# Pairing the third 128-token blocks from the first tile on in a fused attention and MLP kernel

## The chip, the cores and the metric

One core of a Trainium2 chip. The metric is device time in microseconds (us) of one execution. "Median" is over several executions, with the range behind it. "Span" is the profiled time from the first to the last instruction, some 2 us less. The granted clock is the share of TensorE's full clock that the profile records as granted: 1.00 is full, 0.50 half. All runs timed in rounds count as fast ones.

## The reference, cut to what matters

```python
# attention (RWKV-6): batch 4, heads 8, sequence 768, head size 48
for t in range(S):
    cur = einsum('bhd,bhe->bhde', u * k_t, v_t)
    y[:, :, t] = einsum('bhd,bhde->bhe', r_t, state + cur)
    state = w_t[..., None] * state + einsum('bhd,bhe->bhde', k_t, v_t)
x = y.transpose(0, 2, 1, 3).reshape(3072, 384)
# MLP: w_in is 384 x 2048, w_out is 2048 x 384
out = gelu_exact(x @ w_in) @ w_out
```

All is fp32. The kernel works through the 3072 tokens in eight tiles of T = 384, so three blocks of 128 tokens each.

## The kernel before: the parts that matter

While the MLP of tile x-1 runs, step by step, the attention of tile x is issued between its steps, in "slots". `place` says after which MLP step each slot comes; `place_next` does the same for the first two slots of tile x+1. In the traces an engine runs its own instructions in the order of issue (in `shift`, below, TensorE stood from 143.90 us on for two GELUs, and these ran only at 145.57, behind copies at which ScalarE had stood 3.76 us), so `place` sets who waits for whom.

```python
for x in range(1, NX):
    place = [1, 3, ..., 26, 32] if x == 1 else [1, 6, 8, 13, 15, 16, 18, 18, 20, 21]
    place_next = [38, 47] if x == 1 else [21, 24] if x % 2 == 0 else [25, 27]
    ...
    for step, _ in enumerate(mlp(x - 1)):
        if x == 1 and step == 2 * NF - 2:
            make_quarter_masks()
            more = w_sums()          # eight VectorE sums of w_out, needed from tile 1 on
        next(more, None)
        ...                          # weight conversion, loads of tile x + 1
        while place and place[0] <= step:
            place.pop(0)
            next(slots, None)
```

The second layer of the MLP multiplies two blocks at once in the manner of Strassen: seven products of eight matmuls of half width (128x192; in the profile before 56 of them take 18.21 us, 0.325 us each), where the plain way takes 32 matmuls of 128x384 (16 take 10.32 us, 0.645 us each), worth eight products. The first two blocks of a tile are paired with each other (not in tile 0, where the sums of `w_out` are not ready). The third blocks are paired over two tiles. The earlier tile "waits": it multiplies its block in two products. The later one "ends" the pair in five.

```python
def mlp(x):
    waits, ends = x % 2 == 1 and x < NX - 1, x % 2 == 0 and x > 0
    ...
    if final:           # tile 7: its third block alone, 16 matmuls of 128x384
        ...
    if halves:          # tiles 1 to 7: first two blocks, seven products
        ...
    if waits:           # two products on the third block
        ...
    elif ends:          # five more, and the results of both third blocks
        ...
    elif not final:     # tile 0: two blocks plainly, then the third alone
        ...
```

The "quarter products" L521 of tile 2 read `kx`, which VectorE's L500 writes last, after copies of ScalarE (L494):

```python
plain(FINE)             # ScalarE, L494
lay_out(FINE)           # VectorE, L499 and L500
yield                   # the slot at step 6 ends here; the products come at step 8
for h in QUARTERS:
    ...                 # TensorE: L514, then L521
```

A later slot transposes k: VectorE writes blocks (L473), twelve transfers of 48 KB move them (L468, eight issued by SyncE, four by ScalarE), and the k-v products (L598) read them.

## Time and profile before

| | before |
|---|---|
| time, median of 3 (range) | 604.82 us (604.36 to 607.17) |
| span of the profiled run | 601.6 us |
| mean granted TensorE clock | 1.000 |
| TensorE, VectorE, ScalarE busy | 98%, 78%, 30% |

Busy shares are averages over stages with different limits. Up to about 110 us VectorE converts the weights and is the bound (busy 9.76 to 9.86 of each 10 us from 60 to 110). From 170 us on TensorE runs with hardly a gap (none over 0.6 us in this profile).

### The profile page before, as it was taken

The numbers are of one execution on the slowest core, as the hardware profiler recorded it, in microseconds if no ns is written. First come the engines' busy times: TensorE is split into PE (matmuls) and PEld (weight loads), VectorE is DVE, ScalarE is ACT, GpSimd is POOL, SyncE is SP. The second block draws the span as 40 slices with busy tenths as digits, with TensorE's granted clock in tenths as the row PEclk, the third lists the DMA queues.
The fourth block names the chain that finished last, engine by engine and source line by source line (L and its number), as shares of the span: only waits on it lengthen the run. The fifth ranks groups of instructions, "written<-read, shape, count | busy, mean of one in ns | idle before, by whom it ended". The sixth has DMA issues, their size and how long they took to land.

```text
span 601.6 us, 16117 instructions
## 1 busy us (share of the span) xinstructions
PE 586.7 (98%) x6993; PEld 455.5 (76%) x7008; DVE 468.4 (78%) x896; ACT 178.9 (30%) x414; POOL 8.4 (1%) x24
## 2 busy tenths in 40 slices
PE   8779999999999999999999999999999999999997
PEld 4556566656798669986699568995689668999977
DVE  8979999998866978488884987679786888665701
ACT  2446476213223322213222232113222133024400
POOL 3100000000000000000000000000000000000000
PEclk9999999999999999999999999999999999999999
DMA  5775348111141305203052304213052002010000
GB/s 201 253 239 194 110 162 297 38 46 60 25 123 45 92 2 111 73 21 93 1 112 73 99 1 83 87 36 92 3 111 73 8 1 40 16 38 8 1 14 26
DMA packets 50566, 46.72 MB, mean 78 GB/s; under 512 B 31680, under 2 KB 35904, under 8 KB 50496
## 3 DMA queue, kind: packets, MB, share of 16 engines
q1 hardware_dynamic: 33152, 29.31, 15.8%
q10 hardware_dynamic: 17344, 16.39, 10.1%
q8 instruction: 55, 0.90, 0.6%
q14 instruction: 15, 0.12, 0.1%
HBM read 36.24 MB, written 4.72 MB: 68 GB/s over the span
## 4 chain that ended last, share of the span: by engine, by line
PE 71%; DMA 1%; issue 0%; DVE 0%; ACTq 0%
PE o_ps L888 30%; PE h_ps L874 26%; PE b L828 5%; PE d L521 4%; PE o_ps L917 2%; PE kv_ps L598 2%; PE y_ps L639 2%; PE y_ps L677 1%; DMA rkw<-kx 1%; PE d L514 1%; DVE o_sb L960 0%; ACTq L468 0%
## 5 line engine op out<-in xcount | busy, mean ns | idle before, releaser
L874 PE MATMUL h_ps<-xT,w_in_sb 128*128 128x384 f32 x672 | 223.0, 489 | 0.0
L874 PEld LDWEIGHTS h_ps<-xT,w_in_sb 128*128 128x128 f32 x672 | 125.9, 190 | 84.6 <-ACT xT L684 0.4
L877 ACT ACTIVATE g<-h_ps 128x384 f32<-128x384 f32 (+1 forms) x112 | 49.4, 443 | 168.3 <-PE h_ps L874 168.3
L888 PE MATMUL o_ps<-t,s 128*128 128x192 f32 x480 | 81.9, 329 | 0.0
L888 PEld LDWEIGHTS o_ps<-t,s 128*128 128x128 f32 x480 | 77.8, 190 | 0.7
L552 DVE COPY_PREDICATED a_sb<-quarter,d 128x384 f32<-128x384 uint8 (+2 forms) x108 | 45.1, 438 | 2.5
L888 PE MATMUL o_ps<-w_out_sb,g 128*128 128x192 f32 x224 | 38.7, 326 | 0.0
L888 PEld LDWEIGHTS o_ps<-w_out_sb,g 128*128 128x128 f32 x224 | 37.0, 190 | 1.9
L613 DVE SCALAR_TENSOR_TENSOR st<-st,tot_sb,kv_ps 128x48 f32<-128x48 f32 x160 | 29.0, 259 | 4.1 <-PE kv_ps L598 4.1
L1011 PE MATMUL o_ps<-w_out_sb,g 128*128 128x384 f32 x96 | 32.2, 491 | 0.0
L888 PE MATMUL o_ps<-w_out_sb,s 128*128 128x192 f32 x160 | 28.3, 330 | 0.0
L888 PE MATMUL o_ps<-t,g 128*128 128x192 f32 x160 | 27.6, 326 | 0.0
L408 PEld LDWEIGHTS d<-rkw 64*64 64x64 f32 x1152 | 18.6, 134 | 11.8 <-DVE rkw L443 7.8
L1011 PEld LDWEIGHTS o_ps<-w_out_sb,g 128*128 128x128 f32 x96 | 17.8, 190 | 12.3 <-DVE o_sb L1017 0.6
L345 DVE TRANSPOSE_TENSOR_REDUCE rkw<-kx 128x48 f32<-128x1536 f32 (+3 forms) x24 | 26.8, 1155 | 0.2
L521 PEld LDWEIGHTS d<-kx,rkw 64*64 64x64 f32 x1152 | 24.3, 133 | 3.4 <-DVE a_sb L559 1.6
L521 PE MATMUL d<-kx,rkw 64*64 64x96 f32 x1152 | 26.5, 245 | 0.0
L888 PEld LDWEIGHTS o_ps<-t,g 128*128 128x128 f32 x160 | 26.3, 190 | 0.0
L888 PEld LDWEIGHTS o_ps<-w_out_sb,s 128*128 128x128 f32 x160 | 25.9, 190 | 0.4
L408 PE MATMUL d<-rkw 64*64 64x64 f32 (+1 forms) x1152 | 20.9, 221 | 4.6 <-DVE rkw L443 2.9
L534 DVE TENSOR_TENSOR rkw<-rkw,tot_sb 128x768 f32<-128x768 f32 x12 | 11.5, 958 | 17.4 <-PE d L521 17.4
L381 DVE TENSOR_TENSOR rkw<-rkw 128x384 f32<-128x384 f32 (+2 forms) x24 | 23.6, 1004 | 0.4
(148 smaller groups left out, 741.8 us busy)
## 6 DMA issues: line engine op xcount, KB each, us to landing
rkw<-in_rkw_dram ACTq DMA_DIRECT2D x45, 256.0 KB, 2.8
raw<-in_w_out_dram SPq DMA_DIRECT2D x8, 768.0 KB, 4.4
out_dram<-o_sb SPq DMA_DIRECT2D x21, 192.0 KB, 1.9
raw<-in_w_in_dram SPq DMA_DIRECT2D x5, 768.0 KB, 6.0
v_in<-in_v_dram ACTq DMA_DIRECT2D x5, 584.0 KB, 3.7
raw<-in_w_in_dram SPq DMA_DIRECT2D x9, 256.0 KB, 3.8
rkw<-in_rkw_dram SPq DMA_DIRECT2D x8, 288.0 KB, 3.4
rkw<-in_rkw_dram SPq DMA_DIRECT2D x9, 256.0 KB, 7.5
```

What stands on the lines that cost most here:

```text
L345: nc.vector.tensor_reduce(out=fine_sb[:, e, 0:n].rearrange("p a n -> p (a n)"), in_=kx[:, o:o + n * n_m].rearrange("p (m j) -> p m j", j=3 ...
L381: nc.vector.tensor_mul(z, z, by)
L408: nc.tensor.matmul(d[half[p], g, n * width:(n + 1) * width], lhsT=kc[half[g], b, i, p], rhs=right(half[g], b, i, p), start=True, stop=True)
L521: nc.tensor.matmul(d[half[p], g, i * 3 * C // 2:(i + 1) * 3 * C // 2], lhsT=kc[half[g], (n + i) // NI, (n + i) % NI, p], rhs=rx[half[g], 2 ...
L552: nc.vector.copy_predicated(out=an[:, :, :, :, (a + 1) * h:], mask=mask.to_broadcast(data.shape), data=data)
L598: nc.tensor.matmul(kv_ps[half[g], p, i * D:(i + 1) * D], lhsT=k_t(b, i, p, g), rhs=vs(b, i, g)[half[p], 0:D], start=True, stop=True)
L613: nc.vector.scalar_tensor_tensor(out=stq[:, q, c], in0=stq[:, q, c - 1] if c else b4[:, q, NC - 1], scalar=totq[:, q, c:c + 1], in1=kvs[q ...
L828: nc.tensor.matmul(o, lhsT=lhsT, rhs=rhs, start=start and i == 0, stop=(i == len(factors) - 1), skip_group_check=True)
L874: nc.tensor.matmul(h_ps, lhsT=w_in_sb[:, f // FI, j, f % FI * 128:(f % FI + 1) * 128], rhs=xT[:, j, :], start=(j == 0), stop=(j == NJ - 1))
L877: nc.scalar.activation(out=gs[group][:, f % FG, 0:t], in_=h_ps[:, 0:t], func=AF.Gelu)
L888: nc.tensor.matmul(o, lhsT=lhs(j), rhs=rhs(j), start=start and j == 0, stop=(j == HF - 1), skip_group_check=True)
L1011: nc.tensor.matmul(o, lhsT=block(i, f // HF, f % HF), rhs=w_out_sb[:, f, :], start=(f == 0), stop=(f == NF - 1))
```

## The change

The intent: the third blocks of tiles 0 and 7 are multiplied alone, 16 full matmuls each. If tile 0 pairs with 1, 2 with 3 and so on, no block is alone, and the two cost seven products instead of eight. Tiles 1 to 6 swap roles, tile 0 now waits and tile 7 ends a pair. So the slots, the loads of tile 2, the sums of the weights (which now run over into the next tile) and the sums for the last tile are moved too. The diff, cut:

```diff
-            if i < 3:
-                yield
+            yield                        # h_sums: the last four adds get a slot of their own
...
-        waits, ends = x % 2 == 1 and x < NX - 1, x % 2 == 0 and x > 0
+        waits, ends = x % 2 == 0, x % 2 == 1
...
-        if final:                        # tile 7's third block alone: gone
...
+        else:                            # tile 0: two blocks plainly, 16 steps
+            ...
         if waits:                        # now also in tile 0
-            _, o2, o1 = psum(), psum(), psum()
+            if halves:
+                psum()
+            o2, o1 = psum(), psum()
...
-        elif not final:                  # tile 0's third block alone: gone
...
+    more = iter(())                      # moved out of the loop below
     for x in range(1, NX):
-        place = [..., 18, 20, 26, 32] if x == 1 else [1, 6, 8, ...]
-        place_next = [38, 47] if x == 1 else [21, 24] if x % 2 == 0 else [25, 27]
+        place = [..., 18, 20, 24, 28] if x == 1 else [1, 6, 8, ...]
+        place_next = [30, 33] if x == 1 else [25, 27] if x % 2 == 0 else [21, 24]
...
-        more = iter(())
...
-                for _ in range({18: 1, 22: 2, 25: 1}.get(step, 0)):
+                for _ in range({18: 1, 20: 1, 22: 1, 23: 1, 24: 1}.get(step, 0)):
                     next(more_h)
```

More of the change, by code (lines that the diff above doesn't have):

```diff
@@ L910, in two_rows @@
             return [wk.tile([128, DM], F32, name="o_sb", bufs=2) for _ in range(2)]
-        if final:
-            o_ps = ps.tile([128, BANK], F32, name="o_ps", tag="mm", bufs=2)[:, 0:DM]
-            order = [f for f in range(NF) if f % HF < HF - 1] + [HF - 1, NF - 1]
-            for n, f in enumerate(order):
-                nc.tensor.matmul(o_ps, lhsT=block(2, f // HF, f % HF), rhs=w_out_sb[:, f, :], start=(n == 0), stop=(n == NF - 1))
-            o_sb = wk.tile([128, DM], F32, name="o_sb", bufs=2)
-            nc.scalar.copy(out=o_sb, in_=o_ps)
-            store(x * T + 256, o_sb)
-            yield
+        row0 = x * T
         if halves:
-            row0 = x * T
             o_sb = two_rows()
@@ L966, in mlp @@
             yield
+        else:
+            o_ps = [ps.tile([128, BANK], F32, name="o_ps", tag="mm", bufs=2)[:, 0:DM] for _ in range(2)]
+            for f in range(NF):
+                for i, o in enumerate(o_ps):
+                    nc.tensor.matmul(o, lhsT=block(i, f // HF, f % HF), rhs=w_out_sb[:, f, :], start=(f == 0), stop=(f == NF - 1))
+                if f < NF - 1:
+                    yield
+            for i, o in enumerate(o_ps):
+                o_sb = wk.tile([128, DM], F32, name="o_sb", bufs=2)
+                nc.vector.tensor_copy(out=o_sb, in_=o)
+                store(row0 + i * 128, o_sb)
+            yield
         if waits:
-            _, o2, o1 = psum(), psum(), psum()
+            if halves:
+                psum()
+            o2, o1 = psum(), psum()
             o_sb = wk.tile([128, DM], F32, name="o_sb", bufs=2)
@@ L1004, in mlp @@
             yield
-        elif not final:
-            for blocks in (0, 1), (2,):
-                o_ps = [ps.tile([128, BANK], F32, name="o_ps", tag="mm", bufs=2)[:, 0:DM] for _ in blocks]
-                for f in range(NF):
-                    for i, o in zip(blocks, o_ps):
-                        nc.tensor.matmul(o, lhsT=block(i, f // HF, f % HF), rhs=w_out_sb[:, f, :],
-                                         start=(f == 0), stop=(f == NF - 1))
-                    if f < NF - 1:
-                        yield
-                for i, o in zip(blocks, o_ps):
-                    o_sb = wk.tile([128, DM], F32, name="o_sb", bufs=2)
-                    nc.vector.tensor_copy(out=o_sb, in_=o)
-                    store(x * T + i * 128, o_sb)
-                yield
     units = [attention(0, unit) for unit in range(units_of(0))]
@@ L1052 @@
     next(slots)
+    more = iter(())
     for x in range(1, NX):
-        place = [1, 3, 5, 7, 9, 11, 13, 15, 18, 20, 26, 32] if x == 1 else [1, 6, 8, 13, 15, 16, 18, 18, 20, 21]
-        place_next = [38, 47] if x == 1 else [21, 24] if x % 2 == 0 else [25, 27]
+        place = [1, 3, 5, 7, 9, 11, 13, 15, 18, 20, 24, 28] if x == 1 else [1, 6, 8, 13, 15, 16, 18, 18, 20, 21]
+        place_next = [30, 33] if x == 1 else [25, 27] if x % 2 == 0 else [21, 24]
         loads = load(x + 1, nc.scalar if x > 1 else nc.sync)
-        times = range(20, 30) if x == 1 else (2, 3, 4, 5, 16, 17, 18, 19, 20, 21)
+        times = range(18, 28) if x == 1 else (2, 3, 4, 5, 16, 17, 18, 19, 20, 21)
         following = attention(x + 1, 0) if x + 1 < NX else iter(())
-        more = iter(())
         for step, _ in enumerate(mlp(x - 1)):
```

## The prediction

> **What bounds the kernel now.** I began with the page: the busy shares, then the 40 slices.

> ```profile
> PE 586.7 (98%) x6993; PEld 455.5 (76%) x7008; DVE 468.4 (78%) x896; ACT 178.9 (30%) x414; POOL 8.4 (1%) x24
> ...
> PE   8779999999999999999999999999999999999997
> ...
> DVE  8979999998866978488884987679786888665701
> ```

> TensorE is busy 98% of the span, but VectorE is at 9 tenths until about 120 us (slice 8 of 15 us) as well. So the program has two regimes, and a saved matmul is worth something only in the second. The chain of work that ended last, in order of time, says where the second begins and what it consists of:

> ```profile
> 166.78 3.37 DMA rkw<-kx
> 170.16 0.14 issue
> 170.29 1.73 PE kv_ps L598 x92
> ...
> 541.06 28.60 PE b L828 x176
> 569.66 10.32 PE o_ps L917 x32
> 579.98 18.21 PE o_ps L888 x112
> 598.20 0.02 issue
> 598.22 0.36 DVE o_sb L960
> ```

> From 170.29 to 598.20 us it is TensorE with hardly a gap; before it stands a transfer (tile 2's transposed k), fed by VectorE. "x" counts records, two per matmul. So the alone block of the last tile is 16 matmuls of 128x384 in 10.32 us, 0.645 us each, and the paired products are 56 matmuls of 128x192 in 18.21 us, 0.325 us each. (The means of the group rows, 489 and 326 ns, are not spacings: they count half matmuls that overlap.)

> For the first regime I read the timeline of VectorE and of TensorE between 95 and 165 us.

> ```profile
> 110.80 0.69 DVE L262 TENSOR_TENSOR quarter<-p,u 128x48 uint8<-128x48 int32 x6
> 111.42 0.95 DVE L727 TENSOR_TENSOR t<-w_out_sb 128x768 f32<-128x768 f32 x1
> 112.52 1.20 DVE L1017 COPY o_sb<-o_ps 128x384 f32<-128x384 f32 x2 [0.15 <-PE o_ps L1011]
> ...
> 119.72 3.01 DVE L358 SCALAR_TENSOR_TENSOR kx<-rkw,u_sb,rkw 128x384 f32<-128x384 f32 x4
> 122.76 1.78 DVE L345 TRANSPOSE_TENSOR_REDUCE rkw<-kx 128x48 f32<-128x1536 f32 x1
> 125.51 0.56 DVE L1017 COPY o_sb<-o_ps 128x384 f32<-128x384 f32 x1 [0.97 <-PE o_ps L1011]
> 125.99 0.95 DVE L377 TENSOR_TENSOR tot_sb<-rkw 128x768 f32<-128x768 f32 x1
> ...
> 142.41 0.96 DVE L500 TENSOR_TENSOR kx<-kx,tot_sb 128x768 f32<-128x768 f32 x1 [0.40 <-ACT kx L494]
> ...
> 160.09 1.96 DVE L473 STREAM_TRANSPOSE kx<-rkw 128x384 f32<-128x384 f32 x4
> ```

> ```profile
> 115.53 9.94 PE L1011 MATMUL o_ps<-w_out_sb,g 128*128 128x384 f32 x30
> 125.31 17.58 PE L874 MATMUL h_ps<-xT,w_in_sb 128*128 128x384 f32 x54
> 142.82 1.06 PE L514 MATMUL d<-rkw 64*128 64x48 f32 x16
> 143.81 2.21 PE L521 MATMUL d<-kx,rkw 64*64 64x96 f32 x96
> ```

> The reader is to see a near tie: the 27 first-layer matmuls of tile 1 (17.4 us from 125.3) and L514 end at 143.8, and VectorE's L500, which the L521 products read, ends at 143.37. TensorE is 0.4 us the later. If TensorE came earlier, it would wait for VectorE.

> [...]

> **The change part by part.**

> *Arithmetic.* Before, the third blocks of tiles 0 and 7 were multiplied alone: 2 x 16 matmuls of 0.645 = 20.6 us. After, they too are paired by seven products of eight half-width matmuls: 56 x 0.325 = 18.2 us. TensorE loses 2.4 us of work. Tiles 1 to 6 swap roles (two alone products in even tiles, five in odd ones) and keep their sum, three of each.

> *Where the work goes.* Tile 0 loses 10.32 and gains 16 x 0.325 = 5.2 us: 5.1 less in the first regime. Tile 7 loses 10.32 and gains 40 x 0.325 = 13.0 us: **2.7 more at the very end**, where TensorE sets the time. So the gain must come out of the first regime.

> *The first regime.* VectorE's order up to the last weight conversion (110.2 us) stays. TensorE then stands thus: the two fence copies free tile 1's y products (L677) at about 110.5; they now come before the last six matmuls of the pair of blocks, which end about 110.5 + 1.6 + 6 x 0.645 = 116.0. In VectorE's new order the first slot of tile 2's attention (L358 and L345, 4.8 us) comes before the copies of the pair: 112.4 + 4.8 = 117.2. The alone products need those two banks. They run from about 117.9, when the first copy is done, to 123.1. The add that finishes them (now L980) stands ahead of the second attention slot: VectorE, done with two weight sums at about 119 to 120, waits for it some 3 us. Then comes the fourth weight sum (0.87), and the second slot starts at about 124.4 instead of 125.99. But the other four weight sums (L727), which before were done by 119.7, now lie between it and L500: 4 x 0.87 = 3.5 us. L500 ends at 124.4 + 17.4 + 3.5 = 145.3, perhaps 0.4 less if the wait for ScalarE goes: 144.9 to 145.3 against 143.4. TensorE would have been there at 123.1 + 18.4 = 141.5 and waits. So L521 runs at 145.0 to 145.4 instead of 143.8, and everything to the transpose, its transfer and the kv products moves with it: **about 1.4 us later**, instead of 5.1 earlier.

> *The last handover.* Tile 6 now ends with the two alone products. The differences of tile 7's inputs (four adds of 0.36 us) are issued on VectorE behind the add that waits for the last of them. The second matmul of the last tile needs the first two. After the last product: 0.36 + 0.27 + 0.36 and about 0.2 for semaphores (an estimate from the 0.27 us between the same adds at 536 us), less the 0.33 us of the one matmul that can run: TensorE stands **about 0.85 us**. Before, those adds lay two products ahead of the end (535.98 to 537.3, the last tile from 540.9).

> *The last store* is 96 KB instead of 192: medians 1.6 and 1.9 us to landing in the table of DMA issues, so 0.3 less. The extra sums of tile 7 (eight of 0.68 us) lie beside products of 2.6 us; in tile 2 the same sequence took 15.80 us for 48 matmuls, 0.2 over 48 x 0.325, so they hide.

> Sum: + 1.4 + 2.7 + 0.85 - 0.3 = + 4.6 us; 604.8 + 4.6 = 609.4.

> **The rivals.**

> *The arithmetic alone.* If TensorE set the pace throughout, the time would fall by 2.4 to 602.4. For it: PE at 98%, and no idle over 0.7 us since 65 us. Against it: VectorE is busy 9.73 to 9.86 of each 10 us from 60 to 120, and the tie at 143.4 to 143.8.

> *VectorE hides part of it.* If the alone add did not hold VectorE up (TensorE further ahead than I think), L500 would end no later than before, and the first regime would give 0 to 1 us. Then + 2.7 + 0.85 - 0.3, less that: 607 to 608. For it: my bank wait hangs on 116 against 117.2, two nearly equal estimates.

> *A new wait in the steady tiles.* The longer tile now hosts the attention of even tiles, the shorter that of odd ones, which has 48 y products instead of 40. xT must be there 7.8 us after L677 ends. Before, in tile 1, the ScalarE copies ended 5.0 us after it (188.1 against 183.1), so some 2.8 us are spare. If they were not, three handovers could cost a few us: 612 to 615. I think it unlikely.

> **Range and chances.** The centre is 609.4. The arithmetic rival sets the low side, the second lies between, the third the high side; runs of one kernel spread by about 2.8 us. The range is 605.0 to 612.5. Two per cent is 12 us, far more than any part here moves: faster 0.01, same 0.97, slower 0.02.

> **What would show each step.** In the timeline after: (1) the copies of the pair's outputs start after L345, at 116 to 118 us, with TensorE idle before the alone products; (2) VectorE idles 2 to 3.5 us before the add L980; (3) TensorE waits 3 to 4 us at the first L521 of tile 2, for L500, which runs at 144 to 146; (4) the kv products of tile 2 start at 171 to 172.5 instead of 170.3; (5) TensorE stands 0.6 to 1.2 us near the start of the last tile; (6) the products after the last first layer take 31.2 us instead of 28.5. If kv starts before 169 us, the first regime was bound by TensorE and I am wrong; if it starts as I say and the end is off, it is the steady tiles or the handover.

## The result and the profile after

| | before | after |
|---|---|---|
| median (range), same chip | 604.59 us (603.91 to 607.17), 4 runs | 614.11 us (611.70 to 615.15), 4 runs |
| ratio, 95% interval | 1 | 1.0144 (1.0101 to 1.0187) |
| span of the profiled run | 601.6 us | 611.8 us |
| mean granted clock | 1.000 | 0.997 |

A ratio is the mean time of one kernel's fast runs over that of the other's fast runs of the same rounds, so it is not quite the ratio of the medians. The change is within 2%, as predicted, but it costs some 9 us where 4.6 were predicted, and the time is outside the range of 605.0 to 612.5.

First VectorE after the last weight conversion (L316). A row has start, duration, engine, line, operation, output and inputs with shapes, count, and in brackets the idle time before it with what ended that. L358 and L345 are the first slot of tile 2's attention, L966 the copies of tile 0's pair of blocks, L980 the add that finishes its alone products, L727 the sums of weights.

```profile
113.25 0.96 DVE L316 CUSTOM_DVE_ANT_0 w_out_sb<-f,e 128x1536 uint16<-128x1536 uint16 x1
...
116.27 3.02 DVE L358 SCALAR_TENSOR_TENSOR kx<-rkw,u_sb,rkw 128x384 f32<-128x384 f32 x4
119.33 1.78 DVE L345 TRANSPOSE_TENSOR_REDUCE rkw<-kx 128x48 f32<-128x1536 f32 x1
121.03 0.98 DVE L966 COPY o_sb<-o_ps 128x384 f32<-128x384 f32 x2
121.94 0.94 DVE L727 TENSOR_TENSOR t<-w_out_sb 128x768 f32<-128x768 f32 x1
122.80 0.95 DVE L727 TENSOR_TENSOR t<-w_out_sb,t 128x768 f32<-128x768 f32 x1
127.17 0.36 DVE L980 TENSOR_TENSOR o_sb<-o_ps,rkw 128x192 f32<-128x192 f32 x1 [3.42 <-PE o_ps L887]
...
145.37 1.84 DVE L727 TENSOR_TENSOR t<-w_out_sb,t 128x768 f32<-128x768 f32 x2
147.10 0.58 DVE L499 TENSOR_TENSOR kx<-rkw,tot_sb 128x384 f32<-128x384 f32 x1
147.79 0.96 DVE L500 TENSOR_TENSOR kx<-kx,tot_sb 128x768 f32<-128x768 f32 x1
```

And TensorE over the same stretch:

```profile
121.61 5.47 PE L887 MATMUL o_ps<-w_out_sb,rkw 128*128 128x192 f32 x32 [1.52 <-DVE o_sb L966]
126.91 17.58 PE L873 MATMUL h_ps<-xT,w_in_sb 128*128 128x384 f32 x54
144.42 1.06 PE L514 MATMUL d<-rkw 64*128 64x48 f32 x16
148.89 3.50 PE L521 MATMUL d<-kx,rkw 64*64 64x96 f32 x96 [3.41 <-DVE kx L500]
```

The chain of waits that was predicted is all there: the copies behind L345, TensorE idle before the alone products, VectorE idle before L980, the sums between, TensorE waiting 3.41 us for L500. What nobody predicted is in the fourth row: the 96 records of L521 last 3.50 us, and before they lasted 2.21. The table of windows (from and to, us, busy TensorE with the number of records, granted clock, DMA share, GB/s) says why. The kernel after:

```profile
148.00:149.00 1.00, 0.11 (x4) 0.59 0.00 0
149.00:150.00 1.00, 1.00 (x28) 0.50 0.08 16
150.00:151.00 1.00, 1.00 (x33) 0.50 0.00 0
151.00:152.00 1.00, 1.00 (x44) 0.70 0.00 0
```

The kernel before, over its L521:

```profile
144.00:145.00 1.00, 1.00 (x56) 1.00 0.07 16
```

From 148.2 us on, some 0.7 us before the wait ends, TensorE is granted half its clock, for 3.4 us. It does 33 records in one us where it did 56.

The end of the chain of the kernel after, in order of time:

```profile
547.89 0.06 DVE o_sb L980
...
548.17 0.36 DVE tot_sb L763
548.53 0.02 issue
548.55 0.37 DVE tot_sb L764
548.92 0.04 issue
548.97 28.54 PE b L827 x174
577.51 31.21 PE o_ps L887 x192
```

The differences of the last tile's inputs (L763, L764) come behind L980, as predicted, and TensorE stands 0.84 us for them. The last products take 31.21 us.

To see where the time went, I read the same landmarks in four profiles of each kernel (from several sessions) and took the differences. All in us; the means are of the four.

| stretch | before (4 profiles) | after (4 profiles) | mean difference | predicted |
|---|---|---|---|---|
| start to end of weight conversion | 110.23, 111.94, 112.13, 111.10 | 114.21, 111.61, 112.40, 111.11 | +0.98 | 0 |
| from there to tile 2's k-v products | 59.61 in all four | 61.99, 62.33, 62.29, 63.56 | +2.93 | +1.4 |
| from there to the last tile's first layer | 371.06, 369.89, 370.39, 370.44 | 371.44, 371.97, 372.27, 371.54 | +1.36 | 0 |
| first layer of the last tile | 28.60 | 29.71 | +1.11 | +0.85 |
| products after it | 28.68 | 31.36 | +2.68 | +2.7 |
| rest (last add, last store) | 3.39 | 3.05 | -0.34 | -0.3 |
| sum = span | 602.08 | 610.80 | +8.72 | +4.65 |

The last three rows hit. The misses are in the second and third, and perhaps the first.

### The profile page after: what moved, and what is told of

It is laid out like the page before. It is cut to its first block, busy times and chain, and to the rows that moved or that the text cites.

```text
span 611.8 us, 16277 instructions
## 1 busy us (share of the span) xinstructions
PE 590.6 (97%) x7056; PEld 464.4 (76%) x7056; DVE 474.4 (78%) x909; ACT 180.2 (29%) x432; POOL 8.4 (1%) x24
## 4 chain that ended last, share of the span: by engine, by line
PE 79%; DVE 16%; issue 3%; DMA 1%; ACT 1%; DVEq 0%
PE o_ps L887 32%; PE h_ps L873 29%; PE b L827 5%; PE d L521 4%; DVE rkw L443 2%; PE kv_ps L598 2%; DVE e L312 2%; PE d L408 2%; PE warm L196 2%; PE y_ps L677 2%; PE y_ps L639 2%; DVE a_sb L453 1%; DMA rkw<-kx 1%; DVE w_out_sb L316 1%; DVE rkw L381 1%
## 5 line engine op out<-in xcount | busy, mean ns | idle before, releaser
L876 ACT ACTIVATE g<-h_ps 128x256 f32<-128x256 f32 (+1 forms) x112 | 47.7, 428 | 168.1 <-PE h_ps L873 168.1
L887 PE MATMUL o_ps<-t,s 128*128 128x192 f32 x528 | 89.8, 328 | 0.0
L887 PEld LDWEIGHTS o_ps<-t,s 128*128 128x128 f32 x528 | 85.6, 190 | 0.7
L887 PEld LDWEIGHTS o_ps<-w_out_sb,g 128*128 128x128 f32 x224 | 37.0, 190 | 1.6
L521 PE MATMUL d<-kx,rkw 64*64 64x96 f32 x1152 | 27.8, 252 | 3.4 <-DVE kx L500 3.4
L887 PE MATMUL o_ps<-w_out_sb,s 128*128 128x192 f32 x176 | 31.0, 330 | 0.0
L521 PEld LDWEIGHTS d<-kx,rkw 64*64 64x64 f32 x1152 | 25.6, 138 | 6.9 <-issue 5.1
L887 PE MATMUL o_ps<-t,g 128*128 128x192 f32 x176 | 30.4, 326 | 0.0
L887 PEld LDWEIGHTS o_ps<-t,g 128*128 128x128 f32 x176 | 28.9, 190 | 0.0
L887 PEld LDWEIGHTS o_ps<-w_out_sb,s 128*128 128x128 f32 x176 | 28.6, 190 | 0.4
L345 DVE TRANSPOSE_TENSOR_REDUCE rkw<-kx 128x48 f32<-128x1536 f32 (+3 forms) x24 | 26.8, 1157 | 0.2
L534 DVE TENSOR_TENSOR rkw<-rkw,tot_sb 128x768 f32<-128x768 f32 x12 | 11.5, 959 | 18.4 <-PE d L521 18.4
L494 ACT COPY kx<-rkw 128x384 f32<-128x384 f32 x36 | 16.0, 508 | 30.8 <-PE d L521 18.0
L700 ACT COPY xT<-y_ps 48x384 f32<-48x384 f32 x42 | 19.9, 473 | 12.4 <-issue 12.0
```

Of the source, the lines that this page charges most:

```text
L345: nc.vector.tensor_reduce(out=fine_sb[:, e, 0:n].rearrange("p a n -> p (a n)"), in_=kx[:, o:o + n * n_m].rearrange("p (m j) -> p m j", j=3 ...
L494: nc.scalar.copy(out=z, in_=r4[:, :, :, f, :])
L521: nc.tensor.matmul(d[half[p], g, i * 3 * C // 2:(i + 1) * 3 * C // 2], lhsT=kc[half[g], (n + i) // NI, (n + i) % NI, p], rhs=rx[half[g], 2 ...
L700: copy(out=xT[s, pair, :].rearrange("p (i c t) -> p c i t", c=2, t=C), in_=y[s])
L876: nc.scalar.activation(out=gs[group][:, f % FG, 0:t], in_=h_ps[:, 0:t], func=AF.Gelu)
L887: nc.tensor.matmul(o, lhsT=lhs(j), rhs=rhs(j), start=start and j == 0, stop=(j == HF - 1), skip_group_check=True)
```

## The experiments

All kernels gave correct results. In each call, before was run on the same chip: medians 604.39 (first call), 605.17 (second), 604.34 (third) and 604.83 (fourth, one run). The theory at the start: the prediction's mechanisms are right, and what is missing is lost at the same places. The rivals: other places, or chance.

### First call: both kernels again, and the two handicaps one by one

`before_again` and `after_again` are the kernels unchanged. `order` takes VectorE's sums out of the way: four of the eight run at once, ahead of tile 2's first slot, and that slot comes one step later, behind the copies of the pair. `handover` draws the last-tile sums one product earlier.

```diff
 # order
                 more = w_sums()
+                for _ in range(4):
+                    next(more)
...
-        place_next = [30, 33] if x == 1 else ...
+        place_next = [31, 33] if x == 1 else ...
 # handover
-                for _ in range({18: 1, 20: 1, 22: 1, 23: 1, 24: 1}.get(step, 0)):
+                for _ in range({18: 1, 20: 1, 22: 2, 23: 1}.get(step, 0)):
```

> The kernel before, unchanged, against itself: how much of the difference is the run and not the change. In the two traces 4.0 of the 10.2 us of difference in span lie before 114 us, where both kernels issue the same instructions (last conversion of w_out ended at 110.1 before, 114.1 after). If that is chance of the start[...], this profile may show the last conversion anywhere from 109 to 115 us and the times spread over 603 to 609. If it belongs to the changed program, the last conversion ends at 110 +- 0.7 us here again, and the ratio is 1.000 +- 0.003.

> The changed kernel, unchanged. If the early 4 us are chance: ratio to before near 1.009 (610 us: tail 2.7, handover 1.0, reordered first attention 2.0, waits in later tiles 0.8, store -0.3 = 6.2 us) and a profile whose last conversion may be anywhere from 109 to 115. If they belong to the program: ratio 1.014 to 1.017 (613 to 615 us) and the last conversion at 113.5 to 114.5 again.

> Changed kernel with only VectorE's order around the end of tile 0 altered: five weight sums instead of one before the copies of the pair's outputs, and tile 2's first attention slot after these copies. Theory (VectorE's order costs time): the pair's copies follow the pair at once, the add of the alone block doesn't wait, the four late weight sums no longer lie before L500; from the last conversion to the first L521 of tile 2 32.4 us instead of 34.75 (33.7 in the kernel before), no 3.4 us wait of TensorE before it and so no half-speed stretch; kv of tile 2 2.5 to 3.5 us earlier than in the changed kernel, time 2.5 to 3.5 us less. Rival (TensorE's work alone sets the time, the wait is only where slack shows): no change in time beyond 0.5 us.

> Changed kernel with only the four input differences of the last tile issued one step earlier, ahead of the add that waits for the last product of tile 6. Theory: the wait of TensorE at the second matmul of the last tile (0.84 us) goes, time 0.8 to 1.0 us less than the changed kernel of the same rounds. Rival (the input xT itself is late, its transfer or copies): the wait stays, time the same.

| run | median (range) | ratio to before, 95% |
|---|---|---|
| before_again | 605.17 (603.90 to 607.07) | 1.0005 (0.9981 to 1.0029) |
| after_again | 613.61 (611.92 to 614.64) | 1.0139 (1.0114 to 1.0164) |
| order | 610.02 (607.05 to 611.01) | 1.0071 (1.0042 to 1.0099) |
| handover | 613.35 (609.04 to 615.03) | 1.0124 (1.0091 to 1.0157) |

The loss is real. Neither of the two ideas about its early part came out whole: the ratio stayed at 1.0139, though the conversion ended at 111.61 us this time and not at 114.21. So the loss does not hang on the early part. `order` wins back 3.6 us: L521 of tile 2 starts 31.58 us after the conversion instead of 34.66, so the order of VectorE's work in that stretch is worth 3 us. But the wait did not go, as had been expected: TensorE still waits 1.50 us at L521 there, and L521 lasts 3.87 us. A wait half as long cost as much in slow clock here (3.50 us behind the wait of 3.41).

In `handover` the wait of 0.84 us is gone and the first layer takes 28.60 us again, 1.1 less. Yet the time fell by only 0.3: the stretch from tile 2's k-v products to the last tile took 374.02 us, two more than in the kernel after. That was the first sign of a loss that jumps about.

### Second call: the clock, and the late transfers

`warm` puts nine dummy matmuls into the wait. `early` makes the kernel before wait, by issuing L521 of tile 2 two steps earlier. `shift` is `order` with L521 one step later. `kvlate` is the kernel after with the k-v products one product later.

```diff
 # warm (kernel after; warm16 has 16)
             for h in QUARTERS:
                 m, r4, t4, s0, s1, s2 = views(h)
+                if x == 2 and h == FINE:
+                    keep_warm(9, True)      # bf16, 128x512, results unused
 # early (kernel before)
-   ... else [1, 6, 8, 13, ...]
+   ... else [1, 6, 6 if x == 2 else 8, 13, ...]
 # shift (on top of order)
+   ... else [1, 6, 9 if x == 2 else 8, 13, ...]
 # kvlate (kernel after)
-   ... 18, 18, 20, 21]
+   ... 18, 18, 21, 22]
```

> The changed kernel with nine dummy matmuls (128x512, bf16) put on TensorE just ahead of the first quarter products of tile 2, where TensorE waits 3.4 us for VectorE. Theory (the wait lets the granted clock fall to 0.50 for about 3.4 us, and the first products L521 last 3.50 to 3.87 us in place of 2.21): with TensorE busy in the wait the clock stays at 1.00 there, the 96 products last 2.2 us again, kv of tile 2 comes 60.5 to 61.2 us after the end of the weight conversion (62.06 and 62.82 in the two profiles of the changed kernel), and the time is 1.3 to 1.7 us below the changed kernel's 613.6, about 612. Rival (these products are slow for another reason, such as their operands or the banks they write): L521 stays at 3.5 to 3.9 us and the time stays at 613.6, or rises if the dummies delay the products.

> The kernel with four weight sums moved ahead (run order, 610.0), and the quarter products of tile 2 one step of the first layer (six rows of 0.337 us, 2.0 us) later, so that TensorE has work where it waited 1.50 us. Theory (the wait costs its own length and the half clock costs 1.6 us more): no wait, L521 at 2.2 us, kv of tile 2 2.5 to 3.1 us earlier after the conversion's end than in order (59.26), so 56.2 to 56.8, and the time near 607. Rival (what follows on VectorE, the scaling after these products, sets kv, so that a gain of TensorE is given back at the second quarter products or at kv): kv stays at 58.5 to 59.3 and the time at 609 to 610.

> The changed kernel with the k-v products and the scan after them one product of eight matmuls (2.6 us) later in tiles 2 to 7. Theory (the transposed-k transfers land 0.3 to 1.7 us too late for the k-v products in three or four of the tiles, in all 1.2 to 3 us more than in the kernel before): with 2.6 us more they are always landed, every stretch from the second quarter products to the end of k-v shows one and the same length, 15.62 + 2.6 = 18.2 us, and the time falls by 1.0 to 2.0 us, to about 612. Rival (the output of the scan then reaches the next tile's first layer too late in the tiles with two products, and TensorE waits there): a new wait before the first layer of tiles 2, 4 or 6, and the time 613.6 to 617.

> The kernel before, with the first quarter products of tile 2 two steps of the first layer (4.0 us) earlier, so that TensorE must wait there as in the changed kernel: L521 is ready 0.4 us before its turn now, so a wait of about 3.5 us. Theory (wait plus half clock): granted clock 0.50 for about 3.4 us after the wait, L521 at 3.5 to 3.9 us in place of 2.21, kv of tile 2 4.8 to 5.3 us later than the 59.6 to 60.1 us after the conversion's end, and the time near 609.5 (before: 604.4). Rival (the slow L521 belongs to the changed kernel alone): the wait of 3.5 us, L521 at 2.2, and the time near 608. A second point, independent of these: if the early part (start to the end of the conversion, 110.2 and 111.9 us in two profiles of the kernel before, 111.6 to 114.2 in four of changed ones) depends on the program, this one should show 110 to 112.

| run | median (range) | ratio to before, 95% |
|---|---|---|
| warm | 613.15 (610.57 to 615.29) | 1.0115 (1.0074 to 1.0157) |
| shift | 609.77 (607.72 to 613.99) | 1.0078 (1.0038 to 1.0117) |
| kvlate | 614.83 (612.04 to 617.41) | 1.0152 (1.0114 to 1.0190) |
| early | 609.83 (609.08 to 613.13) | 1.0078 (1.0042 to 1.0114) |

**early** settles that the slow clock belongs to the wait and not to the changed program. Its TensorE, and the windows after its wait:

```profile
145.51 3.50 PE L521 MATMUL d<-kx,rkw 64*64 64x96 f32 x96 [3.48 <-DVE kx L500]
```

```profile
145.00:146.00 1.00, 0.49 (x12) 0.50 0.00 0
146.00:147.00 1.00, 1.00 (x33) 0.50 0.07 16
147.00:148.00 1.00, 1.00 (x36) 0.50 0.00 0
```

The old kernel with a wait of 3.48 us shows the same half clock and the same 3.50 us. Its k-v products come 64.45 us after the conversion, 4.84 later than 59.61 (expected 4.8 to 5.3), and the time is near the expected 609.5.

**warm** missed. I had taken a dummy for 0.38 us (the profile after has 379 ns as the length of one record); at full clock nine took 2.10 us, and 1.43 us of idle time were left:

```profile
144.51 2.10 PE L196 MATMUL warm<-zeros 128*128 128x512 bf16 x9
146.55 1.06 PE L516 MATMUL d<-rkw 64*128 64x48 f32 x16
149.04 3.87 PE L523 MATMUL d<-kx,rkw 64*64 64x96 f32 x96 [1.43 <-DVE kx L500]
```

(L523 is L521, two lines lower.) So the test did not test, though it shows that 1.43 us was enough for the half clock in this run.

**shift** missed (its k-v products came 60.51 us after the conversion, later than the 59.26 of `order`), and its reason is worth a look. TensorE's and ScalarE's rows:

```profile
146.10 3.88 PE L873 MATMUL h_ps<-xT,w_in_sb 128*128 128x384 f32 x6 [2.20 <-ACT g L876]
```

```profile
140.07 0.49 ACT L876 ACTIVATE g<-h_ps 128x384 f32<-128x384 f32 x1 [1.44 <-PE h_ps L873]
144.32 1.34 ACT L494 COPY kx<-rkw 128x384 f32<-128x384 f32 x3 [3.76 <-DVE rkw L381]
145.57 0.86 ACT L876 ACTIVATE g<-h_ps 128x384 f32<-128x384 f32 x2
```

I had moved the products but not ScalarE's copies that feed them. ScalarE stood 3.76 us at the copies L494, which wait for VectorE; behind them stood the GELUs that free the first layer's two banks. So the step I gave TensorE had to wait for ScalarE, 2.20 us, and met the half clock itself.

**kvlate** did not give -1 to -2: its median lies 1.2 us above that of `after_again`, which is within the intervals. The trace says more than the times. Its k-v products waited less (1.3 us in sum), but the output of the scan came late, as the rival said: TensorE waited 1.08 us for ScalarE in tile 1's products and 0.58, 0.41 and 0.21 us before later first layers. (Its waits at k-v did not all go: tiles 3 and 5 kept 0.5 and 0.8.) So moving this slot lost more than it gave.

### What distinguishes the tiles that wait for transfers

The third row of the table grows because the k-v products of some tiles find the transposed k not landed. They last 1.61 us without a wait. In the kernel after, tiles 2 to 5 wait, in sum 1.5 to 2.4 us in its four profiles (mean 1.9); in the kernel before 0 to 1.2 (mean 0.6), in tiles 2 and 4 alone. That difference, 1.3 us, is the third row's +1.36. Tile 3 in the kernel before, and then in the kernel after, where it takes 2.31 us from first to last:

```profile
235.46 1.61 PE L598 MATMUL kv_ps<-v_in,rkw 64*64 64x48 f32 x96
```

```profile
249.40 0.32 PE L598 MATMUL kv_ps<-v_in,rkw 64*64 64x48 f32 x4
250.01 1.69 PE L598 MATMUL kv_ps<-v_in,rkw 64*64 64x48 f32 x92 [0.29 <-DMA rkw<-kx]
```

I then looked at the DMA queues in the 10 us ahead of each k-v group. The three us in the midst of the twelve transfers in tile 3 of `order` (its k-v products waited 1.29 us for them, and SyncE and ScalarE each had one issue of 1.7 and 2.3 us there, where the others took 0.6 to 0.8):

```profile
DMA  0037888409047788889878988300010001000100
...
q8 instruction: 1, 0.02, 3.1%
```

Each digit is the busy share of the DMA engines in one of 40 slices. One packet of a queue that the profile marks "instruction" falls into them. Over 17 profiles (all but `kvlate`, whose k-v products are moved) and six tiles each, I counted whether a q8 or q14 "instruction" packet lay in the stretch from 8.5 to 4.5 us ahead of the k-v products:

| | k-v waited over 0.1 us | did not wait |
|---|---|---|
| packet in the stretch | 41 | 26 |
| none | 0 | 35 |

I chose the stretch after seeing the data: with 8.5 to 5.5 us, which the expectation of `pad` below names, 8 of the 41 waits have no packet in it. So this is a suspicion with good evidence, and no more. The page of the kernel after counts 7056 matmuls and 7056 weight loads on TensorE, together 14112, and 56 packets of q8, together 0.92 MB: one packet for 252 of them. That of the kernel before has 14001 and 55, one for 255. So I took q8's packets to carry TensorE's instructions, an estimate from these counts and from the mark, and I call packets so marked fetches below. If it is right, they should move when instructions are put in front.

### Third call: the clock again, the fetches, and a repaired version

`warm16` fills the wait whole. `pad` puts 48 more instructions on TensorE at the very start. `best` joins `order` and `handover` with a corrected `shift`: copies and products both one step later. `bestpad` is `best` with the pad.

```diff
 # pad
-    keep_warm(8)
+    keep_warm(2)
+    keep_warm(30, width=128)      # 24 matmuls and 24 weight loads more, about as long
 # best (on top of order and handover)
-   ... else [1, 6, 8, 13, ...]
+   ... else [1, 7 if x == 2 else 6, 9 if x == 2 else 8, 13, ...]
```

> The same as the run warm with 16 dummy matmuls in place of 9. In warm the nine lasted 2.10 us (0.233 us each), left TensorE idle for 1.43 us, and the clock still fell to 0.50. Theory (an idle time of 1.4 us before them is what lowers the clock): 16 last 3.7 us and fill the wait of 3.4 us whole, the clock stays at 1.00 and L521 lasts 2.2 us in place of 3.5 to 3.9; time 1.3 to 1.7 us lower than the changed kernel's 613.6 unless the k-v products wait longer for transfers than there. Rival (these products are slow for another reason): L521 at 3.5 to 3.9 us whatever runs before them.

> The changed kernel with 24 more dummy matmuls at the very start (30 of 128 columns in place of 6 of 512, about equally long), so 48 more instructions on TensorE ahead of everything else and nothing else changed. What the traces so far show: the k-v products wait for their transfers only in tiles in which a packet of the queue of instruction fetches (q8, or q14) moves 8.5 to 5.5 us before them, in the midst of the twelve transposed-k transfers; the changed kernel has one there in tiles 2, 3, 4 and 5, the kernel before in tiles 2 and 4. Theory (the fetches fall at fixed places in TensorE's instructions and hold up the transfers): the q8 packets come 48 instructions earlier, in tiles 2, 3 and 5 some 11 to 13 us before the k-v products, and the waits there (0.35 to 0.57, 0.67 to 0.69 and 0 to 0.86 us) are gone; tile 4 keeps 0.5, or gets it from the q8 packet that now lies 3 us before k-v and would come to 7; the time falls by 1.0 to 1.9 us, to 611.7 to 612.6. Rival (the coincidence is one of place alone, and the transfers are late because of the other work of this stage): the waits stay in tiles 2, 3 and 5 and the time stays at 613.6.

> The changed kernel with all that the runs so far suggest: four weight sums moved ahead as in order, the sums for the last tile one product earlier as in handover, and in tile 2 both the copies that feed the quarter products and the products themselves one step later (in the run shift only the products were later, and ScalarE, which sits in L494 waiting for VectorE, held up the first layer's GELUs, so TensorE waited 2.20 us for it, lost what the shift gave and met the half clock there). Theory: no wait of TensorE between 125 and 160 us, L521 at 2.2 us, kv of tile 2 about 3 us earlier after the conversion's end than in order (59.26), near 56.3; the end 0.84 us sooner for the handover; so 610.0 less 3 less 0.8, near 606.2. Rival (VectorE's own chain to the second quarter products or the transfers set kv of tile 2): kv at 58 or later, and the time at 608.5 to 610.

> The kernel best with the 48 instructions of pad at the start. Theory: waits for the transposed-k transfers in tiles 2, 3 and 5 (0.14, 1.7 and 0.5 us in order) gone, so 1.5 to 2.5 us below best, near 604.2, level with the kernel before (604.4 to 605.2). Rival (fetches do not matter): level with best.

| run | median (range) | ratio to before, 95% |
|---|---|---|
| warm16 | 610.40 (608.35 to 611.46) | 1.0085 (1.0060 to 1.0110) |
| pad | 614.14 (612.73 to 614.91) | 1.0145 (1.0119 to 1.0171) |
| best | 605.00 (602.86 to 606.93) | 1.0005 (0.9987 to 1.0023) |
| bestpad | 607.77 (605.39 to 610.42) | 1.0045 (1.0021 to 1.0070) |

**warm16** confirms the clock theory from the other side. Sixteen useless matmuls in the place of the wait:

```profile
140.88 3.62 PE L196 MATMUL warm<-zeros 128*128 128x512 bf16 x16
144.43 1.06 PE L516 MATMUL d<-rkw 64*128 64x48 f32 x16
145.43 2.21 PE L523 MATMUL d<-kx,rkw 64*64 64x96 f32 x96
```

L521 starts just when it did (34.66 us after the conversion, against 34.66 to 34.68 in the kernel after), but lasts 2.21 us. All six runs had a mean clock of 1.000, and the time is 3.2 us below that of `after_again` and 3.7 below that of `pad` in the same call. The k-v products come at 60.68 instead of 61.99 to 63.56, 1.07 later than in the kernel before: that is the wait without the slow clock. The fall of 3.2 is more than the 1.3 to 1.7 expected; the fourth call tells part of why.

**pad** failed as a way to save time and was useful as a test. The median is 614.14 where 611.7 to 612.6 was expected. The fetch in tile 2 went out of the stretch, and the k-v products there went from 1.96 us (after) to

```profile
175.86 1.61 PE L599 MATMUL kv_ps<-v_in,rkw 64*64 64x48 f32 x96
```

while tile 6, which never waited in the four profiles of the kernel after, got a fetch 6 us ahead of its k-v products (at 448.3 us; the kernel after has one at 454.4, behind the start of its own) and with it

```profile
454.22 2.07 PE L599 MATMUL kv_ps<-v_in,rkw 64*64 64x48 f32 x96
```

(`warm16`, with 32 TensorE instructions more, shows the same in tile 6: a fetch 5.1 us ahead and a wait of 0.4 us.) Tiles 3 and 5 kept a fetch, 8.5 us ahead instead of 6, and a wait. The waits moved and their sum grew (2.6 us), so the time did not fall. `bestpad` agrees in part: nothing in tiles 2 and 3, where the fetches were gone, 0.9 us in tile 4, and none in tile 6 in spite of a fetch. So in these profiles every wait has a fetch in the stretch, but not every fetch has a wait. Whether the fetch holds the transfers up, and how, is open. In time `bestpad` missed: it is 2.8 us above `best`, where 1.5 to 2.5 below was expected. It lost them early. Its profile has a slow clock at 33.9 to 37.3 us, after TensorE had stood 1.25 us in its early attention, and its conversion ends at 115.48 us, 3.7 later than in `best`; from there to the end both take 490.2 to 490.3. All its eight runs have a mean clock of 0.997.

**best** puts the k-v products where they were expected, to a tenth, and its time is 1.2 us better than the 606.2 expected:

```profile
123.27 19.58 PE L873 MATMUL h_ps<-xT,w_in_sb 128*128 128x384 f32 x60
142.78 1.06 PE L514 MATMUL d<-rkw 64*128 64x48 f32 x16
143.78 2.21 PE L521 MATMUL d<-kx,rkw 64*64 64x96 f32 x96
...
168.19 0.32 PE L598 MATMUL kv_ps<-v_in,rkw 64*64 64x48 f32 x4
```

No wait at L521, L521 at full speed (2.21 us), and k-v 56.37 us after the conversion (expected near 56.3): 3.2 us before the old kernel's 59.61. With +2.68 at the tail, -0.32 at the last store and +0.4 in the middle, it ends 490.3 us after the conversion against a mean of 490.7 in the kernel before. All but 0.7 us of the nine are back, and the new pairing is level with the old. No version beat the old kernel measurably.

### Fourth call: four more looks, for the early part

No edit: each kernel twice more, one profile each. Six of the first ten runs of the kernel after have a mean clock of 0.994 instead of 0.997, and no profile had shown where.

> The changed kernel unchanged, one more profile. Open point: six of its ten runs so far have a mean granted clock of 0.994 and take 613.2 to 615.2 us, four have 0.997 and take 611.7 to 613.6; all its profiles so far are of the second kind and show one stretch at 0.50, at the first quarter products of tile 2. If a profile falls on the first kind, a second stretch at 0.50 of about 3.5 us should be seen. Theory A: it lies in the first 110 us, as in the profiles of warm and shift (40 to 47 us), which the change does not touch, so it is chance. Theory B: it lies behind 110 us, at another wait that the change made. The end of the weight conversion: 110.2 to 112.2 us in the three profiles of kernels with the old pairing, 110.8 to 114.2 in those of the new pairing without a low clock there; if the difference is chance, the two ranges should overlap more with more profiles.

> The kernel before, one more profile, for the end of its weight conversion (110.2 and 111.9 us so far) and for a stretch at a low clock: most of its runs have a mean clock of 1.000 or 0.999, some 0.994 to 0.997 at 605 to 608 us. If the early part does not depend on the program, it should also reach 112.5 us or more in one of two further profiles.

> The changed kernel once more, for the same as look_a1: a second stretch at a granted clock of 0.50 in the first 110 us (theory A) or behind them (theory B) if its mean clock is 0.994, and the end of the weight conversion between 110.8 and 114.2 us.

> The kernel before once more, for the same as look_b1: the end of its weight conversion, expected between 110 and 113 us, and a low clock in the first 110 us if its mean clock is under 0.999.

The times were 612.87 and 612.25 us (after), 604.59 and 603.64 (before). `look_a2` has the mean clock of 0.994, and both theories were wrong. There is no second stretch; the one at L521 is twice as long:

```profile
145.00:146.00 1.00, 0.23 (x7) 0.50 0.00 0
...
150.00:151.00 1.00, 1.00 (x2) 0.50 0.00 0
151.00:152.00 1.00, 1.00 (x3) 0.60 0.00 0
```

From 145.0 to 151.8 it is 6.8 us at half clock, twice the 3.4 of the others, and its k-v products come at 63.56, 1.3 later than in `look_a1`. So in these profiles the slow clock comes in lengths of about 3.4 us, one or two at a time. Over all runs of the kernel after, five with 0.997 took 612.4 us on average and seven with 0.994 took 614.1. Of 52 runs of the kernel before, 40 had 0.999 or more (mean 604.4 us) and 12 less (607.0). That is part of why `warm16` gained 3.2 over `after_again`, in which four of six runs had a mean clock of 0.994 and so, as `look_a2` suggests, had paid twice.

The early part (before 110.23 to 112.13, after 111.11 to 114.21) overlaps. (`early`, also the old pairing, has 112.24.) The +0.98 in the table rests on one profile of 114.21 and is not shown to belong to the change.

## Why the prediction was wrong

Its checks, in its own numbering (one reading of the page was short: VectorE's row stays at 9 up to slice 9, some 135 us, not 120; nothing rests on it):

1. Copies behind L345, TensorE idle before the alone products: right. They start 6.8 us after the conversion (predicted 117.2 against 110.2, so 7.0), idle 1.52 us. That a copy on VectorE waits for what was issued ahead of it was my assumption; the trace before shows only the program order. In the profile after it held: the pair's last product ends at 120.09 us, and the copies start at 121.03, at the end of L345.
2. VectorE idle before L980: 3.42 us, in the range of 2 to 3.5.
3. TensorE's wait at L521: 3.41 us, in the range of 3 to 4. L521 came 1.08 us later than before, relative to the conversion, where the sum had 1.2 to 1.6.
4. k-v of tile 2: **wrong**. Expected 1.4 us late, it came 2.4 to 4.0 late (mean 2.93). It started at 176.20 us in the profile, where 171 to 172.5 was said. Counted from the conversion that range is 60.8 to 62.3, and the four profiles have 61.99 to 63.56.
5. The handover: 0.84 us of wait, as predicted; the first layer grew by 1.11.
6. The products after the last first layer: 31.21 us in the chain, predicted 31.2.

The step that failed is "everything to the transpose, its transfer and the kv products moves with it". It moved, and then lost more: behind the wait that I had predicted myself, L521 ran at half clock. I priced a wait of TensorE by its length alone. The slow stretch came on top, here 1.3 us in one profile (2.38 late, of which 1.08 come from the later L500) and 2.9 in another (`look_a2`). `early` shows this in the old kernel, `warm16` removes it in the new one: there k-v is 1.07 us late, so the predicted path is right, its 1.4 was 0.3 too high, and the clock is the term that was left out.

The second failure is a term of zero. I counted the steady tiles as unchanged and looked there only for late inputs of the first layer, my third rival. That rival is refuted: no profile of the kernel after shows TensorE waiting there. They lost 1.36 us at another place, the k-v products, which wait for transposed k in more tiles than before. The waits go with fetches among the transfers, and in the kernel after these fall among the transfers of tiles 3 and 5 too (6.5 and 5.9 us ahead of the k-v products in its first profile), where in the kernel before they did not. The coincidence is shown, and that padding moves the waits; that the fetches cause them, and why the transfers stall, is not.

Of the 4.1 us between the predicted 4.65 and the measured 8.72, the first failure is 1.5 and the second 1.4. Another 1.0 lies in the early part and is not shown to belong to the change, and 0.3 in the last tile's first layer, which grew by more than its wait.

The rival "VectorE hides part of it" was refuted by points 1 to 3: the add did hold VectorE up, by 3.42 us. The rival "arithmetic alone" (602.4) was refuted for the kernel as changed. `best` is close to what remains of it: with the waits repaired, the first regime does give 3.2 us, and the tail takes 2.7 of them back.

## What to carry to other kernels

Ask in which stage a saved matmul lies. Here 5.1 us of matmuls (an estimate, 10.32 less 16 of 0.325) left a stage that waits for VectorE, and the k-v products behind it still came 2.93 us later (mean of four profiles); 2.7 us were added at the very end, where TensorE is the bound, and it grew by 2.68. When a change makes a busy TensorE wait, count the wait with and without a slow stretch behind it: here waits of 1.43 to 3.48 us were followed, though not all of them and not in every run, by 3.4 or 6.8 us at half clock. Read the granted clock in windows, not as a mean: 0.997 was all that the mean showed of it. When one slot is moved, look at what stands in front of and behind its companions on the other engines' queues: the copies that were left in place cost the `shift` all its gain (a wait of 2.20 us).
